# A gated-state attention with a low-rank mixer: order of the first batch, its idle products, and of the loads up to unit 5

## The chip, the cores and the metric

One NeuronCore of a Trainium2 chip. The metric is the device time of one execution in microseconds (us). A core has five engines with an instruction stream each: TensorE (PE; its weight loads are shown apart as PEld), VectorE (DVE), ScalarE (ACT), GpSimd (POOL) and SyncE (SP), which here only issues DMA transfers.

## What is computed

```python
f = 1 / (1 + exp(-f_logit))                     # (B, H, S, D) = (4, 8, 768, 48)
for t in range(S):
    state = f[:, :, t, :, None] * state + k[:, :, t, :, None] * v[:, :, t, None, :]
    y[:, :, t] = q[:, :, t] @ state             # per batch and head
x = y as (B, S, H*D) = (4, 768, 384)
u = x + ((x.T @ U) @ V).T                       # U: (768, 32), V: (32, 768), mixes the 768 positions
out = u + relu(u @ w_ch1) @ w_ch2               # 384 -> 1536 -> 384
```

All in float32, except that the four weight matrices come in as float64.

## The kernel before

The attention runs over 16 units, two heads of one batch each; units 0 to 3 are batch 0, units 4 to 7 batch 1, and so on. The 768 positions are cut into 12 chunks of 64, taken two at a time as 6 blocks of 128. Within a chunk the recurrence becomes products: q times the product of gates from the chunk's start (Y), k times the inverse of it or the product to its end (X), a masked score matrix, and a state handed from chunk to chunk by a scan on VectorE.

For units 0 to 3 the gates are worked out through logarithms. `prepare(n)` gives five pieces, which `front(n, ...)` calls by the names gates, read_back, keep, keys, queries:

- `logs` ("gates"): VectorE bounds the f tile (L697), ScalarE takes Exp (L698) and Ln (L699), over all six blocks at once.
- `log_sums` ("read_back"): TensorE multiplies each block with the constant `later`, six products of 130 columns (L705, twelve instructions).
- `keep_logs` ("keep"): ScalarE makes X (L717), Y (L718) and two small tiles from the sums.
- `keys` and `queries`: TensorE transposes k or q (L678), VectorE multiplies with X or Y (L690).

`attend(n)` gives the second half, which `rear(n, ...)` calls: kept (transposes of kz, L864, and ScalarE's copy kb, L868), spread (L874), states (products with v, L885, and the copy `added`, L892), scores (L837), mask (L850), scan (L907), read (q times the states, L924), inner (scores times v, L942, and the copy into x, L948).

The mixer follows for each batch: the low-rank part (L217 to L248 for batch 0), turn (L261 and L262), the first product pz with its relu on ScalarE (L273, L283), and the second. Mixer work of batch 0 runs beside units 4 to 8, and likewise later; from batch 1 on the second product is done with fewer multiplications.

Weights come as float64, in tiles of 384 KB. For each, SP issues the load (L82, a tile `w_raw`, of which there are four, or `zw`), ScalarE splits it (L91, L92), VectorE shapes it in three steps (L98 to L100) in the tile `w_y`, of which there are two, and GpSimd adds the parts (L101). In the list `weights`, 0 to 2 are U and V (`early` is 3), 3 to 14 the twelve tiles of w_ch1, then twelve of w_ch2. `ahead_by(early + FIRST, weights)` issues the load nine places ahead of the tile that is converted.

The order on TensorE, VectorE and ScalarE is the program's order throughout (`manual_schedule`); SP's order is the program's until `written.close()`. `load(n, names)` issues the loads of unit n: two transfers of 144 KB for each of f, k and q (L563), and three for v (L563, L556). Units 0, 2, 4 use the slots in `late`, units 1, 3, 5 those in `other`; there are three v tiles. `busy(n)` issues idle products that nothing reads. In `late`, slice 3 is `ends`, slices 4 and 5 are X of units 0 to 3 in turn.

Of the kernel before, what the change touches and what calls it, by code (L numbers as in the profile page):

```python
# [14 lines left out]
AF = mybir.ActivationFunctionType  # L15
# [12 lines left out]
FLOOR = -40.0  # L28
# [459 lines left out]
def factored_path(ctx, tc, q, k, v, f_logit, moe_U, moe_V, moe_w_ch1, moe_w_ch2, out, ok):  # L488
# [82 lines left out]
                        in_=head[:, :, part * NB : part * NB + n_ch],  # L571
                    )

    load(0, "f")
    load(1, "f")
    load(0, "k", "q", "v")

    nc.scalar.preload_act_table_set("natural_log_exp_and_others")

# [81 lines left out]
    def prepare(n):  # L661


        T = units[n] = {}
        b = n // HP
        r, f = raw[n % 2], fz[n % 2]
        by_chunk = f[:, 0:S].rearrange("p (c t) -> p c t", t=C)

        def follow(nm):

            if n >= HP and n + 2 < NU:
                load(n + 2, nm)

        def on_tensor(nm):

            pt = ps_big.tile([P, 2, 512], F32, name="pt", tag="big")
            for c in range(NBL):
                nc.tensor.transpose(  # L678
                    pt[:, 2 * c // NBL, c % (NBL // 2) * P : (c % (NBL // 2) + 1) * P],
                    nat[n % 2][nm][:, c].rearrange("p h d -> p (h d)"), ident,  # L680
                )
            return pt[:, :, 0 : G * C].rearrange("p a (c t) -> p a c t", t=C)

        def halves(t):
            return t[:, 0:S].rearrange("p (a c t) -> p a c t", a=2, t=C)

        def operand(nm, of):
            t = T[nm] = kz[n % 2][:, C:] if nm == "k" else two.tile([P, S], F32, name="qT")
            if n < TURNED:
                nc.vector.tensor_tensor(halves(t), on_tensor(nm), halves(T[of]), ALU.mult)  # L690
            else:
                turned(t, r[nm])
                nc.vector.tensor_tensor(t, t, T[of], ALU.mult)

        def logs():
            fn = nat[n % 2]["f"][:, :, :, 0:D]
            nc.vector.tensor_single_scalar(fn, fn, FLOOR, ALU.max)  # L697
            nc.scalar.activation(fn, fn, AF.Exp, scale=-1.0)  # L698
            nc.scalar.activation(fn, fn, AF.Ln, bias=1.0)  # L699

        def log_sums():
            pt = T["sums"] = ps_big.tile([P, 2, 512], F32, name="pt", tag="big")
            for c in range(NBL):
                o = c % (NBL // 2) * (P + 2)
                nc.tensor.matmul(  # L705
                    pt[:, 2 * c // NBL, o : o + P + 2],
                    lhsT=nat[n % 2]["f"][:, c].rearrange("p h d -> p (h d)"), rhs=later, start=True, stop=True,
                )

        def keep_logs():  # L710
            by_block = T["sums"][:, :, 0 : NBL // 2 * (P + 2)].rearrange("p a (c t) -> p a c t", t=P + 2)

            def blocks_of(t):
                return t.rearrange("p (a c t) -> p a c t", a=2, t=P)

            T["X"], T["Y"] = late[:, 4 + n % 2, :], fz[n % 2][:, 0:S]
            nc.scalar.activation(blocks_of(T["X"]), by_block[:, :, :, 0:P], AF.Exp, scale=-1.0)  # L717
            nc.scalar.activation(blocks_of(T["Y"]), by_block[:, :, :, 0:P], AF.Exp)  # L718
            nc.scalar.activation(
                least[:, n, :].rearrange("p (a c s) -> p a c s", a=2, s=2), by_block[:, :, :, P : P + 2], AF.Exp, scale=-1.0  # L720
            )
            nc.scalar.copy(wholes[n % 2][:, 1:NCH], least[:, n, 1:NCH])

        def gates():
            f0 = T["f0"] = two.tile([P, NCH], F32, name="f0")
            if n < TURNED:
                pt = on_tensor("f")
                nc.scalar.activation(halves(f)[:, :, :, 1:C], pt[:, :, :, 1:C], AF.Sigmoid)
                nc.scalar.activation(f0.rearrange("p (a c) -> p a c", a=2), pt[:, :, :, 0], AF.Sigmoid)
                follow("f")  # L730
                return
            fT = late[:, 6, :]
            turned(fT, r["f"])
            follow("f")
            fv = fT.rearrange("p (c t) -> p c t", t=C)
            nc.scalar.activation(by_chunk[:, :, 1:C], fv[:, :, 1:C], AF.Sigmoid)  # L736
            nc.scalar.activation(f0, fv[:, :, 0], AF.Sigmoid)

        def keep():
            X = T["X"] = late[:, 4, :]  # L740
            nc.vector.tensor_tensor_scan(  # L741
                backwards(X, S - 1, S), backwards(f, S, S), backwards(ends, S - 1, S), 0.0,
                ALU.mult, ALU.add,
            )
            X0 = X.rearrange("p (c t) -> p c t", t=C)[:, :, 0]
            nc.scalar.copy(least[:, n, :], X0)
            X1 = two.tile([P, NCH], F32, name="X1")
            nc.vector.tensor_single_scalar(X1, X0, LEAST, ALU.max)
            nc.vector.reciprocal(starts.rearrange("p (c t) -> p c t", t=C)[:, :, 0], X1)
            whole = wholes[n % 2]  # L750
            nc.vector.tensor_tensor(whole[:, 1:NCH], T["f0"][:, 1:NCH], X0[:, 1:NCH], ALU.mult)

        def keys():
            operand("k", "X")
            follow("k")

        def read():
            Y = T["Y"] = late[:, 5, :]
            nc.vector.tensor_tensor_scan(Y, f[:, 0:S], starts, 0.0, ALU.mult, ALU.add)  # L759

        def queries():
            operand("q", "Y")
            follow("q")

        if n < HP:
            return [logs, keep_logs, keys, log_sums, queries]
        return [gates, keep, keys, read, queries]
# [190 lines left out]
    def front(n, *names):  # L958

        if n >= NU:  # L960
            return []
        if n not in ahead:
            ahead[n] = dict(zip(("gates", "keep", "keys", "read_back", "queries"), prepare(n)))
        return [ahead[n].pop(nm) for nm in names]

    def rear(n, *names):

        if not 0 <= n < NU:
            return []
        if n not in here:  # L970
            here[n] = dict(zip(("kept", "states", "scan", "scores", "read", "inner", "mask", "spread"), attend(n)))
        return [here[n].pop(nm) for nm in names if nm in here[n]]
# [53 lines left out]
    with tc.manual_schedule(engines={nc.vector.engine, nc.scalar.engine}):  # L1026
# [1 line left out]

        idle = ps_mm.tile([P, 512], F32, name="idle", tag="mm")

        def busy(n):
            for _ in range(n):
                nc.tensor.matmul(idle[:, 0:DM], lhsT=ident, rhs=ends[:, 0:DM], start=True, stop=True)  # L1033

        written = ExitStack()
        written.enter_context(tc.manual_schedule(engines={nc.sync.engine}))
        busy(2)
        for piece in front(0, "gates", "read_back", "keep"):
            piece()
        load(2, "f")  # L1040
        load(1, "k", "q", "v")
        loads = ahead_by(early + FIRST, weights)
        halves, join = [[w[i] for w in weights[:early]] for i in (2, 3)]
        done, rest = slice(0, 2 * (HP - 1) * D), slice(2 * (HP - 1) * D, DM)
# [10 lines left out]
        for n in range(HP):  # L1055
            last = n + 1 == HP
            pieces = rear(n - 1, "scan", "mask") + front(n, "keys")
            if last:
                pieces += join[:1]
            elif n < 2:  # L1060
                pieces += [lambda: busy(2)]
            pieces += rear(n, "spread") + rear(n - 1, "read") + rear(n, "kept")
            if last:
                pieces += halves[1:2] + front(n, "queries") + rear(n - 1, "inner") + [held] + join[1:2] + rear(n, "states")
                pieces += halves[2:] + rear(n, "scores")
            else:
                pieces += rear(n - 1, "inner") + front(n + 1, "gates") + front(n, "queries") + rear(n, "states", "scores")
                pieces += (halves[:1] if n + 2 == HP else []) + front(n + 1, "read_back", "keep")
            for piece in pieces:
                piece()  # L1070
            if n == 0:
                load(3, "f")
                load(2, "k", "q", "v")
                for load_w in weights[:early]:
                    load_w[0]()
            elif n == 1:
                load(3, "k", "q", "v")
                for load_w in weights[early : early + 2]:
                    load_w[0]()
        m = mixer(0)  # L1080
        low_rank_of, added_up_of, mix_of, warm = m.some
        for piece in rear(n, "scan", "mask") + join[2:]:
            piece()
        load(HP + 1, "f", "k", "q", "v")
        for load_w in weights[early + FIRST : early + FIRST + early]:
            load_w[0]()
        written.close()
        low_rank_of(done)
        warm(2)
        loads[early]()  # L1090
        nc.vector.memset(starts, 0.0)
        for t in fz:
            nc.vector.memset(t, 0.0)
        for piece in rear(n, "read"):
            piece()
        added_up_of(done)
# [6 lines left out]
        mix_of(rest)  # L1103
        warm(3)
        loads[early + 1]()
        loads = loads[early + 2 :]

        start = m.before[3:5] + m.firsts[0:1] + m.before[5:]
# [398 lines left out]
```

## Time and profile before

| | us |
|---|---|
| three runs | 482.61, 483.89, 484.61; median 483.89 |
| profiled execution | 483.7 |
| its span, first to last instruction | 482.0 |
| TensorE busy | 462.7 |
| VectorE busy | 345.3 |
| ScalarE busy | 179.8 |
| GpSimd busy | 36.3 |
| first unit's log sums start | 6.61 |
| first product of the mixer (L273) starts | 49.98 |

The span is what the profile shows; the time of the same execution is 1.7 us longer. A profile line of the timeline has start, length, engine, line of the kernel, operation, the tiles written and read, shapes and count, and in brackets how long the engine sat idle before and what ended it. Matmuls overlap, so lengths of TensorE lines are a little longer than their distance.

### The profile page before, as it was taken

How to read it: one execution, taken by the hardware profiler on the slowest of the kernel's cores; microseconds unless marked ns; L12 is line 12 of the kernel's file. 1: busy time of each engine (PE TensorE's matmuls, PEld its weight loads, DVE VectorE, ACT ScalarE, POOL GpSimd, SP SyncE). 2: the span in 40 equal slices, each digit the busy share in tenths (PEclk: the TensorE clock that was granted, in tenths of full speed). 3: DMA queues.
4: the chain of work that ended last, by engine and by line, in shares of the span. 5: the costliest groups of instructions: out<-in, count | busy, mean ns of one | idle time of the engine just before them, and what ended most of it. 6: DMA issues, size and time to landing. Idle time of an engine off the chain costs nothing.

```text
span 482.0 us, 12801 instructions
## 1 busy us (share of the span) xinstructions
PE 462.7 (96%) x5561; PEld 399.8 (83%) x5561; DVE 345.3 (72%) x555; ACT 179.8 (37%) x335; POOL 36.3 (8%) x48
## 2 busy tenths in 40 slices
PE   6999989999999899999999999999999999999995
PEld 4886877886666468799899888899979999999995
DVE  2568769878999755757766646997896886858642
ACT  4675567573444313424342414542321311212200
POOL 2002435443000000000000000000000000000000
PEclk9999999999999999999999999999999999999999
DMA  9977985658787521153426200100000000000001
GB/s 144 160 161 205 171 234 151 161 132 114 114 122 110 98 42 26 26 75 72 64 29 114 43 31 4 28 3 20 18 0 1 33 2 18 18 0 34 1 33 40
DMA packets 158680, 34.36 MB, mean 71 GB/s; under 512 B 149206, under 2 KB 157078, under 8 KB 158614
## 3 DMA queue, kind: packets, MB, share of 16 engines
q1 hardware_dynamic: 158614, 33.44, 37.3%
q8 instruction: 46, 0.75, 0.7%
q14 instruction: 20, 0.16, 0.1%
HBM read 28.70 MB, written 4.72 MB: 69 GB/s over the span
## 4 chain that ended last, share of the span: by engine, by line
PE 70%; DVE 13%; ACT 4%; DMA 4%; SPq 3%; issue 3%; POOL 1%; DVEq 0%; POOLq 0%; ACTq 0%
PE pw L327 26%; PE pz L273 16%; PE pp L425 12%; PE y L942 2%; DVE late L759 2%; PE sc L837 2%; PE y L924 2%; SPq L569 2%; PE po L298 2%; PE put L261 1%; PE pt L705 1%; DVE added L907 1%; PE pt L864 1%; PE idle L1033 1%; DVE late L741 1%
## 5 line engine op out<-in xcount | busy, mean ns | idle before, releaser
L273 PE MATMUL pz<-uT,w 128*128 128x256 f32 x504 | 114.5, 382 | 4.1 <-ACT z_all L283 3.8
L273 PEld LDWEIGHTS pz<-uT,w 128*128 128x128 f32 x504 | 93.8, 190 | 18.0 <-ACT z_all L283 4.8
L327 PE MATMUL pw<-w,z_all 128*128 128x192 f32 x216 | 37.7, 329 | 0.0
L327 PE MATMUL pw<-zw,w_raw 128*128 128x192 f32 x216 | 37.3, 327 | 0.0
L327 PEld LDWEIGHTS pw<-zw,w_raw 128*128 128x128 f32 x216 | 35.2, 190 | 0.7 <-DVE w_raw L197 0.6
L327 PEld LDWEIGHTS pw<-w,z_all 128*128 128x128 f32 x216 | 35.0, 190 | 0.7
L101 POOL TENSOR_TENSOR w<-w_y,w_r 128x384 int32<-128x384 int32 x24 | 31.7, 1320 | 42.4 <-DVE w_y L100 39.3
L283 ACT ACTIVATE z_all<-pz 128x512 f32<-128x512 f32 x33 | 19.7, 597 | 32.7 <-PE pz L273 32.6
L425 PE MATMUL pp<-v_nat,late 128*128 128x128 f32 x224 | 28.8, 275 | 0.0
L425 PEld LDWEIGHTS pp<-v_nat,late 128*128 128x128 f32 x224 | 27.0, 192 | 0.0
L418 ACT ACTIVATE other<-other 128x512 f32<-128x512 f32 x18 | 11.3, 632 | 39.9 <-DVE other L197 39.9
L912 ACT COPY st<-added 128x576 f32<-128x576 f32 x12 | 14.7, 1225 | 30.5 <-DVE added L907 30.5
L298 PE MATMUL po<-w,z_all 128*128 128x384 f32 x72 | 24.9, 493 | 1.2 <-DVE o L197 1.2
L298 PE MATMUL po<-w,zw 128*128 128x384 f32 x72 | 25.3, 496 | 0.0
L741 DVE TENSOR_TENSOR_SCAN late<-fz,late 128x768 f32<-128x768 f32 x12 | 21.1, 1756 | 4.0 <-ACT fz L736 3.6
L850 DVE TENSOR_TENSOR A<-sc,causal 128x768 f32<-128x768 f32 x16 | 15.1, 946 | 10.8 <-PE sc L837 10.8
L98 DVE TENSOR_SCALAR w_y<-w_y 128x384 f32<-128x384 f32 (+3 forms) x27 | 12.5, 465 | 12.9 <-ACT w_y L91 12.6
L298 PEld LDWEIGHTS po<-w,z_all 128*128 128x128 f32 x72 | 13.3, 190 | 10.1 <-DVE o L197 1.8
L298 PEld LDWEIGHTS po<-w,zw 128*128 128x128 f32 x72 | 13.1, 190 | 9.7 <-issue 1.2
L759 DVE TENSOR_TENSOR_SCAN late<-fz,other 128x768 f32<-128x768 f32 x12 | 21.0, 1747 | 0.2
L418 ACT ACTIVATE z_all<-z_all 128x512 f32<-128x512 f32 x12 | 7.6, 632 | 32.8 <-DVE z_all L197 32.8
L892 ACT COPY added<-ds 48x576 f32<-48x576 f32 (+1 forms) x28 | 17.8, 635 | 3.3 <-PE ds L885 3.2
(215 smaller groups left out, 846.0 us busy)
## 6 DMA issues: line engine op xcount, KB each, us to landing
w_raw<-in_moe_w_ch_dram SPq DMA_DIRECT2D x18, 384.0 KB, 3.4
out_dram<-o SPq DMA_DIRECT2D x24, 192.0 KB, 2.0
v_nat<-in_v_dram SPq DMA_DIRECT2D x16, 144.0 KB, 3.3
v_nat<-in_v_dram SPq DMA_DIRECT2D x32, 72.0 KB, 3.2
zw<-in_moe_w_ch_dram SPq DMA_DIRECT2D x6, 384.0 KB, 5.7
late<-in_f_logit_dram SPq DMA_DIRECT2D x10, 96.0 KB, 3.2
late<-in_k_dram SPq DMA_DIRECT2D x10, 96.0 KB, 2.7
late<-in_q_dram SPq DMA_DIRECT2D x10, 96.0 KB, 2.9
```

The lines of the kernel that those rows point to most:

```text
L101: nc.gpsimd.tensor_tensor(dst.bitcast(I32), shaped(y.bitcast(I32)), shaped(r), ALU.add)
L273: nc.tensor.matmul(pm[:, i * 2 * P : (i + 1) * 2 * P], lhsT=w1[:, m, o : o + P], rhs=uT[a][:, m, :], start=(m == 0), stop=(m == NDC - 1))
L283: nc.scalar.activation(z[a, c][:, k : k + 2, :].rearrange("p i t -> p (i t)"), pm, AF.Relu)
L298: nc.tensor.matmul(pm, lhsT=z[a, i // NI][:, i % NI, s * P : (s + 1) * P], rhs=w2[:, i, :], start=(i == 0), stop=(i == NFC - 1))
L327: nc.tensor.matmul(pm[:, n * HM : (n + 1) * HM], lhsT=lhs[:, i, :], rhs=rhs[:, i, :], start=(i == 0), stop=(i == NI - 1))
L418: nc.scalar.activation(dst, dst, AF.Relu, scale=float(SIGNS[n]))
L425: nc.tensor.matmul(pm[:, i, r * P : (r + 1) * P], lhsT=room["w"](wn)[:, r * P : (r + 1) * P], rhs=x_node(a, xn), start=((xn, wn) == of[0]) ...
L741: nc.vector.tensor_tensor_scan(backwards(X, S - 1, S), backwards(f, S, S), backwards(ends, S - 1, S), 0.0, ALU.mult, ALU.add,)
L759: nc.vector.tensor_tensor_scan(Y, f[:, 0:S], starts, 0.0, ALU.mult, ALU.add)
L850: nc.vector.tensor_tensor(T["A"], sc[:, :, 0 : NBL * C].rearrange("p h (c i) -> p h c i", i=C), causal.unsqueeze(1).unsqueeze(1).broadcast ...
L892: nc.scalar.copy(added[r, 1:].rearrange("p (e c s) -> p e c s", c=NBL, s=2), ds[r, :, 0 : NBL * D].rearrange("p s (c e) -> p e c s", e=D),)
L912: nc.scalar.copy(st, states.rearrange(by_e, c=NCH))
```

## The change

Five things are changed, all in the way from the first load to the first products of the mixer.

1. A tile of zeros, `blank` (slice 5 of `late`, 384 columns), is the first memset of VectorE, and `busy` multiplies it with itself in place of `ident` and `ends`. `busy(3)` stands at the start in place of `busy(2)`; the `busy(2)` in units 0 and 1 goes, and unit 0 gets one idle product of 256 columns.
2. Unit 0's logarithms are taken in two halves of three blocks, and X of unit 0 in two halves.
3. In unit 0, queries, kept and scores come ahead of `log_sums` of unit 1, with the queries straight after the keys, the scores ahead of the states.
4. The loads are in another order: f, k, q of unit 0, then f of unit 1, then v of unit 0; k and q of a unit ahead of f of the next one; U, and V with the second part of `early`, behind unit 2; three weight tiles (list places 9 to 11) ahead of unit 5's loads in place of behind them.
5. The clearing of `starts` and `fz` moves from between the conversions of weights 3 and 4 to behind that of 4.

```diff
+    blank = late[:, 5, 0 : 3 * P]
+    nc.vector.memset(blank, 0.0)
+    load(0, "f", "k", "q")
     load(1, "f")
-    load(0, "k", "q", "v")
+    load(0, "v")
...
         def logs():
-            fn = nat[n % 2]["f"][:, :, :, 0:D]
-            nc.vector.tensor_single_scalar(fn, fn, FLOOR, ALU.max)
-            nc.scalar.activation(fn, fn, AF.Exp, scale=-1.0)
-            nc.scalar.activation(fn, fn, AF.Ln, bias=1.0)
+            m = 2 if n == 0 else 1
+            parts = [nat[n % 2]["f"][:, i * NBL // m : (i + 1) * NBL // m, :, 0:D] for i in range(m)]
+            for fn in parts:
+                nc.vector.tensor_single_scalar(fn, fn, FLOOR, ALU.max)
+            for fn in parts:
+                nc.scalar.activation(fn, fn, AF.Exp, scale=-1.0)
+                nc.scalar.activation(fn, fn, AF.Ln, bias=1.0)
...
-            nc.scalar.activation(blocks_of(T["X"]), by_block[:, :, :, 0:P], AF.Exp, scale=-1.0)
+            for a in (slice(0, 1), slice(1, 2)) if n == 0 else (slice(0, 2),):
+                nc.scalar.activation(blocks_of(T["X"])[:, a], by_block[:, a, :, 0:P], AF.Exp, scale=-1.0)
...
-        def busy(n):
+        def busy(n, cols=DM):
             for _ in range(n):
-                nc.tensor.matmul(idle[:, 0:DM], lhsT=ident, rhs=ends[:, 0:DM], start=True, stop=True)
+                nc.tensor.matmul(idle[:, 0:cols], lhsT=blank[:, 0:P], rhs=blank[:, 0:cols], start=True, stop=True)
...
-        busy(2)
+        busy(3)
         for piece in front(0, "gates", "read_back", "keep"):
             piece()
+        load(1, "k", "q")
         load(2, "f")
-        load(1, "k", "q", "v")
+        load(1, "v")
...
-            elif n < 2:
-                pieces += [lambda: busy(2)]
+            if n == 0:
+                pieces += front(n, "queries") + rear(n, "spread", "kept") + [lambda: busy(1, 2 * P)]
+                pieces += front(n + 1, "gates") + rear(n, "scores", "states") + front(n + 1, "read_back", "keep")
+                for piece in pieces:
+                    piece()
+                load(2, "k", "q")
+                load(3, "f")
+                load(2, "v")
+                continue
...
-            if n == 0:
-                load(3, "f")
-                load(2, "k", "q", "v")
-                for load_w in weights[:early]:
+            if n == 1:
+                weights[0][0]()
+                load(3, "k", "q")
+                for load_w in weights[1:early]:
                     load_w[0]()
-            elif n == 1:
-                load(3, "k", "q", "v")
+                load(3, "v")
                 for load_w in weights[early : early + 2]:
                     load_w[0]()
...
-        load(HP + 1, "f", "k", "q", "v")
         for load_w in weights[early + FIRST : early + FIRST + early]:
             load_w[0]()
+        load(HP + 1, "f", "k", "q", "v")
         written.close()
         low_rank_of(done)
         warm(2)
         loads[early]()
-        nc.vector.memset(starts, 0.0)
-        for t in fz:
-            nc.vector.memset(t, 0.0)
...
         loads[early + 1]()
+        for t in [starts] + fz:
+            nc.vector.memset(t, 0.0)
```

Unit 0's old order on TensorE was keys, two idle products, kept, queries, states, scores, then the log sums of unit 1.

More of the change, by code (lines that the diff above doesn't have):

```diff
@@ L572, in load @@
                     )
-    load(0, "f")
+    blank = late[:, 5, 0 : 3 * P]
+    nc.vector.memset(blank, 0.0)
+    load(0, "f", "k", "q")
     load(1, "f")
-    load(0, "k", "q", "v")
+    load(0, "v")
     nc.scalar.preload_act_table_set("natural_log_exp_and_others")
```

## The prediction

> **What bounds the kernel now.** I read the page's first and second part, then the chain of waits in order of time, then the timelines of TensorE, ScalarE and the SP queue for the first 75 us, and last the waits of TensorE after 48 us.
>
> ```profile
> PE 462.7 (96%) x5561; PEld 399.8 (83%) x5561; DVE 345.3 (72%) x555; ACT 179.8 (37%) x335; POOL 36.3 (8%) x48
> PE   6999989999999899999999999999999999999995
> DMA  9977985658787521153426200100000000000001
> ...
> PE pz L273 <- ACT z_all L283: 3.8, 3, 1.8
> ```
>
> TensorE is the bound: 96% of the span, and after the first batch its waits are few (the last line: three waits, 3.8 us, for the relu that empties the output of the mixer's first product). So TensorE's stream after about 48 us is nearly solid, and whatever is taken away ahead of it, or out of a hole in it, should come off the end one for one. There are two such places: the first batch (0 to 48 us), which is a chain of short steps, and a hole at 62 us.
>
> The first batch, TensorE's timeline (start, length, then what; L705 is the product `log_sums`, once per unit, and so marks the units):
>
> ```profile
> 3.89 2.93 PE L1033 MATMUL idle<-late,ident 128*128 128x384 f32 x4 [3.89 <-POOL ident masks.py:199]
> 6.61 2.79 PE L705 MATMUL pt<-later,late 128*128 128x130 f32 x12
> ...
> 14.67 1.61 PE L705 MATMUL pt<-later,other 128*128 128x130 f32 x12
> ...
> 16.77 1.46 PE L1033 MATMUL idle<-late,ident 128*128 128x384 f32 x4
> ...
> 23.63 1.61 PE L705 MATMUL pt<-later,late 128*128 128x130 f32 x12
> ...
> 31.68 1.61 PE L705 MATMUL pt<-later,other 128*128 128x130 f32 x12
> ```
>
> The reader is to see three things. The first L705 group takes 2.8 us, the later ones 1.6: the same twelve instructions at half pace. The distances of the L705 groups are 8.06, 8.96 and 8.05 us; the long one is unit 1, where idle products stand at 16.77 in front of the read of the states (L924, at 18.15). And TensorE does nothing until 3.89, waiting for `ident` from GpSimd.
>
> The hole, from the timelines of TensorE, ScalarE and SP:
>
> ```profile
> 63.66 5.45 PE L273 MATMUL pz<-uT,w 128*128 128x256 f32 x24 [1.76 <-ACT z_all L283]
> ...
> 73.31 2.86 PE L273 MATMUL pz<-uT,w 128*128 128x256 f32 x12 [0.96 <-ACT z_all L283]
> ...
> 62.13 0.54 ACT L91 ACTIVATE w_y<-w_raw 128x384 f32<-128x384 f32 x1 [5.44 <-DMA w_raw<-in_moe_w_ch_dram]
> ...
> 51.57 1.15 SPq L563 DMA_DIRECT2D other<-in_f_logit_dram  x2
> ...
> 57.74 6.76 SPq L82 DMA_DIRECT2D w_raw<-in_moe_w_ch_dram  x5
> ```
>
> TensorE waits 1.76 us for a relu; ScalarE had waited 5.44 us for a weight tile with the relu queued behind; SP issued that tile at 57.74 because unit 5's loads (51.57 to 57.69) stood ahead of it. The 0.96 us at 73.31 is what is left of the same jam: the relu there stood behind the gates of unit 4, themselves late because ScalarE worked off its queue.
>
> [...] L705 has 0.215 us per instruction until 9.40, the transposes after it 0.11. [...] here the q, k, v, f rows are 192 B and move at about 165 GB/s when several are queued (7 to 9 us), the weight tiles at about 345 (59 to 64 us). So the order of loads matters in the first batch.
>
> **The change part by part.** All against the profiled execution: 483.7 us with a span of 482.0, which is 0.2 below the median of 483.89.
>
> Warm-up. The zero tile is half of L606's columns (0.70 us for 768), so 0.35 on VectorE from 0.90; it delays only VectorE's constants, which end at 2.51 with the engine free until 4.63. Idle products then start at about 1.3 instead of 3.89; six instructions of 0.64 (the pace at 3.89) end at 5.15. [...] I carry both, 2.58 or 1.55 us.
>
> Logarithms in halves. The f tile of unit 0 lands as before (4.63). A half costs VectorE about 0.28 (of 0.46) and an activation 0.40 (L228's copy of 288 columns); so the first half is ready at 5.82, the second at about 6.5, where the whole is ready now at 6.52. Log sums end at 7.4 (warm) or 8.4 (cold) against 9.40. X in halves costs 0.3 more on an idle ScalarE, and the second half ends 0.55 after the sums.
>
> Loads of unit 0. k and q move ahead of unit 1's f. Issue to landing is 4.2 to 4.3 for k: second half now at 7.9, then at about 6.1; q at about 8.0 instead of 9.6; f of unit 1 at 9.7 instead of about 6.6, where it is first used after 9.9. The five loads of 295 KB at 165 GB/s from 2.6 us on still put v of unit 0 at about 12.1, as now.
>
> Queries ahead, filler cut. kz ends at 9.2 (warm) or 10.3 (cold), qT 0.9 to 1.4 later (13.77 now), scores at 11.1 or 12.6. Then `states` needs v: it starts at 12.1 or 12.6, takes 0.75, and unit 1's log sums start at 12.95 (warm) or 13.6 (cold: unit 1's logarithms end then) against 14.74 in the chain. Gain 1.8 or 1.1. What is late next is v's transfer; without it the warm gain would be about 0.9 more.
>
> Unit 1. The two idle products (1.29 us) ahead of L924 go. Its distance should become that of unit 2, 8.05, plus 0.3 because the mask of unit 0 now stands just ahead of kz: unit 2's log sums at 21.3 against 23.70. Gain in all 2.4 warm, 1.7 cold; I take 2.2. Its v (issue about 0.8 earlier, landing about 19.2) is wanted at 19.2; no room, 0.5 if it is late. Units 2 and 3 keep their 8 us. SP's reordering there (U behind unit 2, unit 3's k and q ahead of V) leaves each load before its use by my count: k of unit 3 about 1 us, the others 1 to 2.
>
> Weight tiles between units 4 and 5. SP issues them at 51.5 (49.3 with the shift) instead of 57.74, so they land at about 54.3; ScalarE comes to the first at 56.7 (54.5 shifted). Both 1.76 and 0.96 go: 2.7. Unit 5's six loads and three behind them in kind go back by about 1.8 us of issue; its f is first used by TensorE at 82.6, so nothing is late.
>
> Clearing of `starts` and `fz`. 2.2 us of VectorE (0.70 + 1.51) leave 43.4 to 45.6, where the five additions to x wait for them but TensorE's next transpose doesn't start later for it, and go to 49.6, into the conversion of weights. Two conversion buffers make ScalarE wait for GpSimd; walking the queue I find the copy of the third turned block 0.15 late for TensorE and the rest covered (a product pair takes 2.6 us, a conversion about 2). Cost 0.15, between 0 and 1.
>
> Sum: 2.2 + 2.7 - 0.15 = 4.75; 483.7 - 4.75 = 479.0. Everything after 75 us only moves ahead, since units 4 and on and TensorE's fillers are started by the same stream.
>
> **The rivals.** First, the weights still come late for ScalarE (the queue is fuller when the first batch is shorter, or the cleared tiles cost their 2 us): only the first part stays, 483.7 - 2.2 = 481.5. For it: the landing at 54.3 has only 0.2 us to spare. Against it: a late tile of a few tenths costs only those.
>
> Second, the first batch is held by its transfers: the DMA row stands at 7 to 9 tenths there and v of units 0 and 1 lands just in time. Then only the hole goes: 483.7 - 2.6 = 481.1. Against it: SP waits for free buffers at 8.65 and 16.34 now, which the new order fills.
>
> Third, slower: with the filler cut from 2.58 to 0.43 us in units 0 and 1, TensorE has only 1.9 us of work (kept, filler, scores) between 8.7 and 12.1. [...] a unit's 7.2 us of products take 14.4, 6.4 more than the slack of 0.8 hides. One cold unit gives 479.0 + 6.4 = 485.4, two 491.8; I enter 488. It decides the sign from about 5.3 us of products at half rate on. Against it: TensorE never rests longer than 1.2 us at a stretch in my walk, and no L705 group after the first is slow.
>
> **How the numbers follow.** The forecast 0.60, late weights 0.16, transfers 0.12, the cold clock 0.12. The predicted time is that of the first, 479.0; its own range is 477.0 (v early, warm, no cost of the clearing) to 480.5 (cold start, 0.5 for v, 1 for the clearing). To hold eight in ten I reach to the first two rivals and a little of the third: 476.8 to 483.5. What a measurement here can tell from no change is about 0.5%, 2.4 us: faster below 481.5, slower above 486.3. Faster 0.73 (0.58 + half of each of the first two rivals), within 0.18, slower 0.09.
>
> **What would show it.** Right: a first idle product near 1.3 us; log sums of units 1 and 2 near 13.0 and 21.3; `states` of unit 0 waiting for v; no wait of L273 near 60 us. Wrong: log sums of unit 2 after 22.5, L705 at 0.215 us per instruction in unit 1 or later, a DMA wait of L91 that outlasts 55 us, or new waits of TensorE between 75 and 180 us, which would mean that the vector work and not TensorE set the pace there.

## The result, and the profile after

| | before | changed |
|---|---|---|
| median, us | 483.75 (7 runs, 482.61 to 484.61) | 480.69 (7 runs, 479.83 to 481.94) |
| ratio, 95% interval | | 0.9941 [0.9924, 0.9959] |
| span of the profiled execution | 482.0 | 479.0 |
| log sums of units 1, 2 and 3 start | 14.67, 23.63, 31.68 | 12.92, 22.05, 30.35 |
| first product of the mixer (L273) starts | 49.98 | 49.49 |
| kept of unit 4 done, next L273 starts | 79.86 | 77.03 |

The kernel became 3.1 us faster, by the median, where 4.75 were forecast. The last three rows tell where. Unit 1 starts 1.75 us earlier, as forecast; the gain shrinks to 1.58, 1.33, and to 0.49 at the first product of the mixer, where 2.2 were forecast. Between the first product and 77.03 it grows by 2.34, where 2.55 were forecast, and from there it stays to the end of the span (3.0).

The timeline of TensorE of the changed kernel for the first batch (start, length, engine, line, operation, tiles, shapes, count, and in brackets the idle time before and what ended it):

```profile
1.39 4.21 PE L1039 MATMUL idle<-late 128*128 128x384 f32 x6 [1.39 <-DVE late L575]
6.01 2.09 PE L710 MATMUL pt<-later,late 128*128 128x130 f32 x12 [0.41 <-issue]
...
15.98 1.24 PE L930 MATMUL y<-st,qT 48*64 48x48 f32 x44 [0.80 <-DVE A L856]
...
19.31 1.28 PE L891 MATMUL ds<-v_nat,kb 64*64 64x48 f32 x48
20.59 0.68 PE L843 MATMUL sc<-qT,kz 48*64 48x64 f32 x29
21.56 0.56 PE L843 MATMUL sc<-qT,kz 48*64 48x64 f32 x19 [0.29 <-issue]
...
26.33 1.16 PE L948 MATMUL y<-v_nat,A 64*64 64x48 f32 x48
...
30.35 1.16 PE L710 MATMUL pt<-later,other 128*128 128x130 f32 x8
32.35 0.61 PE L710 MATMUL pt<-later,other 128*128 128x130 f32 x4 [0.83 <-issue]
```

The idle products start at 1.39 and the log sums (L705 of before is L710 here) at 6.01, as forecast. Then look at the groups that are cut in two. The scores of unit 1 stop after 29 of 48 for 0.29 us, the log sums of unit 3 after 8 of 12 for 0.83 us, and "issue" says that nothing the profile shows ended the wait. L948 of unit 2 takes 1.16 where it takes 0.92 elsewhere, and `states` of unit 1 (L891) 1.28 instead of 0.92. The profile of the kernel before has no such gap; these are its scores of unit 1, all 48 in one piece:

```profile
22.77 0.93 PE L837 MATMUL sc<-qT,kz 48*64 48x64 f32 x48 [0.37 <-ACT late L699]
```

But the same first batch was profiled again in the first experiment below, which leaves it as it was, and there these scores do stop, after 25 of 48:

```profile
22.52 0.59 PE L837 MATMUL sc<-qT,kz 48*64 48x64 f32 x25 [0.37 <-ACT late L699]
23.48 0.57 PE L837 MATMUL sc<-qT,kz 48*64 48x64 f32 x23 [0.37 <-issue]
```

So the stop is not a thing of the new order alone, and one profile is one draw. The first product of the mixer starts at 49.98, 50.02 and 50.15 in the three profiles of the old first batch that were taken with all its loads and none added, and anywhere from 49.25 to 50.68 in the six with the changed one. What the first batch is worth is therefore read from the times below, and the 0.49 of this pair of profiles is not taken as its size.

The hole: first the product that ends the stretch in TensorE's timeline of the kernel before (it begins with the one at 49.98), then the timelines of TensorE, SP and ScalarE of the changed kernel:

```profile
79.86 2.86 PE L273 MATMUL pz<-uT,w 128*128 128x256 f32 x12
```

```profile
49.49 2.83 PE L273 MATMUL pz<-uT,w 128*128 128x256 f32 x12 [0.33 <-ACT uT L262]
...
55.72 5.45 PE L273 MATMUL pz<-uT,w 128*128 128x256 f32 x24 [0.15 <-ACT uT L262]
61.01 0.82 PE L680 MATMUL pt<-ident,late 128*128 128x128 f32 x6
61.66 5.35 PE L273 MATMUL pz<-uT,w 128*128 128x256 f32 x24
...
70.48 2.86 PE L273 MATMUL pz<-uT,w 128*128 128x256 f32 x12 [0.23 <-ACT z_all L283]
...
77.03 2.86 PE L273 MATMUL pz<-uT,w 128*128 128x256 f32 x12
```

```profile
51.39 1.68 SPq L82 DMA_DIRECT2D w_raw<-in_moe_w_ch_dram  x3
...
61.78 1.61 SPq L82 DMA_DIRECT2D w_raw<-in_moe_w_ch_dram  x3
```

```profile
57.88 0.57 ACT L91 ACTIVATE w_y<-w_raw 128x384 f32<-128x384 f32 x1 [0.44 <-POOL w L101]
...
66.09 0.55 ACT L91 ACTIVATE w_y<-w_raw 128x384 f32<-128x384 f32 x1 [0.61 <-DMA w_raw<-in_moe_w_ch_dram]
```

The three tiles are issued at 51.39 and ScalarE no longer waits for the first of them; the wait of 1.76 us is gone and that of 0.96 has become 0.23. A new one of 0.15 stands before the third turned block (the clearing, forecast 0.15). Together that is 2.34 less, the whole of what this stretch gained. What is left is the next weight tile, issued at 61.78 behind unit 5's loads, for which ScalarE waits 0.61.

### The profile page after: what moved, and what is told of

Read it like the earlier page. It is cut to its first block, busy times and chain, and to the rows that moved or that the text cites. A ratio compares the mean times of both kernels' runs of the same rounds, so it can differ in the third digit from the quotient of the medians.

```text
span 479.0 us, 12800 instructions
## 1 busy us (share of the span) xinstructions
PE 462.1 (96%) x5557; PEld 399.0 (83%) x5557; DVE 346.0 (72%) x557; ACT 181.0 (38%) x338; POOL 36.1 (8%) x48
## 4 chain that ended last, share of the span: by engine, by line
PE 75%; DVE 11%; ACT 5%; issue 3%; DMA 3%; SPq 1%; POOL 0%; DVEq 0%; ACTq 0%
PE pw L327 26%; PE pz L273 20%; PE pp L425 12%; PE sc L843 2%; PE y L948 2%; PE y L930 2%; DVE late L765 2%; PE po L298 2%; DVE late L747 1%; DVE added L913 1%; PE put L261 1%; PE pt L870 1%; PE ds L891 1%; PE pt L710 1%; PE pu L207 1%
## 5 line engine op out<-in xcount | busy, mean ns | idle before, releaser
L273 PE MATMUL pz<-uT,w 128*128 128x256 f32 x504 | 114.7, 382 | 1.8 <-ACT z_all L283 1.3
L273 PEld LDWEIGHTS pz<-uT,w 128*128 128x128 f32 x504 | 93.7, 190 | 15.8 <-ACT z_all L283 2.1
L327 PE MATMUL pw<-w,other 128*128 128x192 f32 x108 | 18.6, 327 | 0.0
```

Of the source, the lines that this page charges most:

```text
L273: nc.tensor.matmul(pm[:, i * 2 * P : (i + 1) * 2 * P], lhsT=w1[:, m, o : o + P], rhs=uT[a][:, m, :], start=(m == 0), stop=(m == NDC - 1))
L327: nc.tensor.matmul(pm[:, n * HM : (n + 1) * HM], lhsT=lhs[:, i, :], rhs=rhs[:, i, :], start=(i == 0), stop=(i == NI - 1))
```

## The experiments

The theory after the result: (1) the hole and the first batch are two separate gains; (2) units 1 to 3 are held by transfers, so that what unit 0 gains is taken back there. The rivals: that the hole closes only because the batch ends earlier; that the new order of the engines' work stretches the units; that the profiled execution was an unlucky one. All ratios are to the kernel before, run on the same chip beside the experiment.

**The two halves, each alone.** The first has of the change only this:

```diff
-        load(HP + 1, "f", "k", "q", "v")
         for load_w in weights[early + FIRST : early + FIRST + early]:
             load_w[0]()
+        load(HP + 1, "f", "k", "q", "v")
...
-        nc.vector.memset(starts, 0.0)
-        for t in fz:
-            nc.vector.memset(t, 0.0)
...
         loads[early + 1]()
+        for t in [starts] + fz:
+            nc.vector.memset(t, 0.0)
```

> The kernel before with only the three weight tiles ahead of unit 5's loads and the clearing of starts and fz behind weight 4. Theory A (the hole at 62 us is worth its 2.7 us by itself, and the first batch gives next to nothing at its end): 2.3 to 2.7 us less than before, ratio 0.9945 to 0.9955; no wait of L273 over 0.3 us between 55 and 70. Theory B (the hole closes only because the first batch ends earlier, so that the weights and ScalarE fall in step): less than 1.5 us gain.

Measured: 480.86 against 483.73, ratio 0.9942 [0.9924, 0.9961], 2.87 us. The waits that remain in it are 0.16 and 0.32, a little above the bound set. The hole is worth nearly the whole change by itself.

The second is the changed kernel with these lines put back.

> The changed kernel with the weight tiles and the clearing put back where they were before. Theory A (the first batch's gain is lost again in units 1 to 3): 0.2 to 0.8 us less than before, ratio 0.998 to 1.0; log sums of unit 1 near 12.9, first product of the mixer within 0.7 of 49.98; the wait of ScalarE for the weight tile as long as before. Theory B (the 1.8 us at unit 1 reach the mixer in most executions, and the profiled one was unlucky): about 1.5 to 2 us less than before.

Measured: 483.0 against 483.73, ratio 0.9986 [0.9975, 0.9997], 0.73 us; first product at 49.61, 0.37 earlier than before. This is the upper end of theory A, and theory B's 1.5 to 2 is outside the interval. In its profile the log sums of unit 3 again stop after 8 of 12 instructions, for 0.76 us. ScalarE waits 4.81 us for the weight tile at 61.13, 0.6 less than before. The two parts add up to 3.6, the change gave 3.1, within what these intervals can tell.

**A quarter of the first batch's transfers taken away.** In this kernel q of units 0 to 3 isn't loaded; it is set to zero once. The engines do the same instructions, on zeros where q was.

```diff
         for nm in names:
+            if nm == "q" and n < HP:
+                continue
...
-            nc.gpsimd.memset(t[:, :, :, D:PAD], 0.0)
+            nc.gpsimd.memset(t if nm == "q" else t[:, :, :, D:PAD], 0.0)
```

> The changed kernel without the loads of q for units 0 to 3 (their q is set to zero once by GpSimd), so that a quarter of the first batch's bytes and issues is gone and all engines have the same work. Theory A (units 1 to 3 are stretched by transfers: v of unit 1 late[...]): the distances of the log sums fall from 9.13, 8.3 (plus 0.83 inside L710) and 8.2 to about 8.3, 8.05 and 7.2, the first product of the mixer comes 1.3 to 2 us earlier, at about 47.8, and the end with it. Theory B (the new order of the engines' work stretches them: mask ahead of kz, read behind the mask): the distances stay, and the first product stays within 0.5 of 49.5.

Measured: 478.63, ratio 0.9902 [0.9865, 0.9938], 5.1 us below before. TensorE's timeline:

```profile
12.53 1.61 PE L712 MATMUL pt<-later,other 128*128 128x130 f32 x12
...
21.06 1.61 PE L712 MATMUL pt<-later,late 128*128 128x130 f32 x12
...
29.12 1.61 PE L712 MATMUL pt<-later,other 128*128 128x130 f32 x12
...
47.23 2.83 PE L273 MATMUL pz<-uT,w 128*128 128x256 f32 x12 [0.33 <-ACT uT L262]
```

The distances are 8.53 and 8.06, no group is cut, and the first product comes 2.26 us earlier than in the changed kernel. With the transfers out of the way the new order gives what the prediction's walk gave it (8.35 and 8.05). So in the changed kernel it is transfers that stretch the units, and not the order of the engines' work. Of that order only a part remains: the read of the states (L932 in this kernel) still waits 0.80 for the mask, and the first distance is 0.2 over the forecast. The time agrees: 478.63 is 1.9 below that of the changed kernel with the clearing on GpSimd, run beside it (480.53, further down). What the kernel before would gain from the same cut of loads was not run.

**More transfers in the kernel before.** Six loads of 144 KB that nothing reads go into z_all, two behind each of units 0 to 2.

```diff
+        def more(n):
+            for par in range(2):
+                o = (2 * n + par) * NBL * D
+                nc.sync.dma_start(
+                    out=junk[:, o : o + NBL * D].rearrange("p (c d) -> p c d", d=D),
+                    in_=f_logit[B - 1, 2 * n + par].rearrange("(c p) d -> p c d", p=P),
+                )
...
+            if n < 3:
+                more(n)
```

> The kernel before with six more loads of 144 KB (rows of 192 B, into z_all, which is first written at 52 us; nothing reads them), two behind each of units 0 to 2, one and a half times a unit's v. Theory A (units 1 to 3 are held by transfers[...]): 864 KB at 165 GB/s is 5.2 us; the slack of the old order takes some 2, so the first product of the mixer comes 2 to 4 us later than 49.98, with waits of DMA or gaps of TensorE that nothing in the kernel explains. Theory B (the batch is a chain of engines and the queue has room): under 0.7 us.

Measured: 485.86 against 484.17, ratio 1.0062 [1.0038, 1.0086]; first product at 52.09, 2.1 later. The nine runs spread from 485.05 to 489.84. The three longest (488.76 and up) had a mean granted clock of 0.985 to 0.991, the others 0.996 to 0.999; none of the three was profiled, so where they lost it is open. TensorE's timeline of unit 2 in the profiled execution:

```profile
25.34 0.85 PE L678 MATMUL pt<-ident,late 128*128 128x128 f32 x6 [0.28 <-DMA late<-in_k_dram]
...
27.90 0.68 PE L942 MATMUL y<-v_nat,A 64*64 64x48 f32 x30
29.42 0.55 PE L942 MATMUL y<-v_nat,A 64*64 64x48 f32 x18 [0.85 <-issue]
```

Both kinds of loss appear in the old order too with a fuller queue: a tile that comes late (k of unit 2, 0.28 us), and a cut group whose wait nothing names (0.85). (The cut group appeared there once without added loads, as shown above.)

**The unnamed gaps.** Where a group is cut can be counted in TensorE's matmul instructions from the first one on. In the changed kernel the stops come after 345 (29 scores of unit 1) and 596 (8 log sums of unit 3); the extra-loads kernel stops after 472, and the stretched L948 of the changed kernel spans 438 to 486. The distances are 127 and 124. In the first experiment, whose first batch has another order, the 25 scores of unit 1 end after 345 too. The next test was a second profile of the changed kernel, and a kernel that has two matmul instructions fewer at its start: unit 0's logarithms and X whole, and the idle products at the start as before.

```diff
-            m = 2 if n == 0 else 1
+            m = 1
...
-            for a in (slice(0, 1), slice(1, 2)) if n == 0 else (slice(0, 2),):
+            for a in (slice(0, 2),):
...
-        busy(3)
+        for _ in range(2):
+            nc.tensor.matmul(idle[:, 0:DM], lhsT=ident, rhs=ends[:, 0:DM], start=True, stop=True)
```

> The changed kernel once more, for a second profile of it and for the comparison with the next three on one chip. Theory A [...]: gaps again at the 29th of the 48 score instructions of unit 1, about two thirds into L948 of unit 2 or at the 8th of the 12 L710 instructions of unit 3, as long as or shorter than before, and nowhere else without a named cause. Theory B (the gaps are chance): other places. Time 480.7, ratio 0.993 to 0.995.

> The changed kernel with unit 0's logarithms and X whole and the idle products at the start as before (two, with ident). Theory A (transfers hold units 1 to 3): unit 1's log sums come about 1.3 later, near 14.2, but the first product of the mixer within 0.6 of 49.5 and the time within 0.6 us of the changed kernel. Theory B (what unit 0 gains is passed on): 1 to 1.5 us more than the changed kernel.

> The changed kernel with unit 0's logarithms and X whole and the start as before, once more beside the changed kernel. Theory A (transfers take most of unit 0's gain): 0.2 to 0.7 us above the changed kernel. Theory B (passed on in full): 1 to 1.5 us above it.

The kernel with whole logarithms, second profile, TensorE's timeline:

```profile
20.60 0.69 PE L843 MATMUL sc<-qT,kz 48*64 48x64 f32 x31
21.46 0.50 PE L843 MATMUL sc<-qT,kz 48*64 48x64 f32 x17 [0.18 <-issue]
...
29.94 1.38 PE L710 MATMUL pt<-later,other 128*128 128x130 f32 x10
31.87 0.38 PE L710 MATMUL pt<-later,other 128*128 128x130 f32 x2 [0.54 <-issue]
```

The stops have moved from 29 to 31 and from 8 to 10: again after 345 and 596 matmul instructions. Its first profile stopped in the scores after 31 (0.44 us) and not in the log sums. The second profile of the changed kernel stopped after 8 of 12 (0.56 us); its scores were hardly cut but took 1.30, and its L948 of unit 2 took 1.10. The places are thus fixed in the instruction stream, and how long the stop is, or whether there is one, depends on the execution. What holds TensorE there was not shown: the lines put the waits, 0.18 to 0.92 us, down to "issue" alone. The page's third part lists a queue of its own for instructions:

```profile
q8 instruction: 46, 0.75, 0.7%
```

In the changed kernel one of these 46 packets falls between 19.0 and 19.2 and one between 29.6 and 29.8, 2.4 to 2.8 us before the stops end (21.56 and 32.35). That names no cause: in the profile of the kernel before one falls between 20.2 and 20.4, 2.4 to 2.6 us ahead of the scores at 22.77, which are not cut.

The time of these kernels: the changed one again 480.22, 0.9933 [0.9911, 0.9956]; whole logarithms 481.79 against 484.17, 0.9959 [0.9945, 0.9974], and in the second series 480.4, 0.9938 [0.9919, 0.9958]. Beside the changed kernel that is 0.2 us slower, by the first series some 0.8, between its two theories; halves and early start are worth something between 0.2 and 0.8, and the intervals can't say where. In the first profile unit 1's log sums start at 14.06 and the first product at 49.81: 1.14 us later than in the changed kernel at unit 1, 0.32 later at the mixer. One reason for such differences is seen in the log sums of unit 0: with the start as before they take 1.64 us in the second profile of this kernel and 2.76 in the first; what decides between the two the profiles don't show. The early start doesn't ensure the shorter time either: 1.70 to 2.94 us over the profiles that have it. In the slowest of them, that of the last experiment below, unit 1's log sums start at 14.32 instead of 12.92.

**The order of the loads in units 1 to 3.** The changed kernel with the order of before for units 1 to 3, U and V:

```diff
-        load(1, "k", "q")
         load(2, "f")
-        load(1, "v")
+        load(1, "k", "q", "v")
...
-                load(2, "k", "q")
                 load(3, "f")
-                load(2, "v")
+                load(2, "k", "q", "v")
+                for load_w in weights[:early]:
+                    load_w[0]()
...
-                weights[0][0]()
-                load(3, "k", "q")
-                for load_w in weights[1:early]:
-                    load_w[0]()
-                load(3, "v")
+                load(3, "k", "q", "v")
```

> The changed kernel with the loads of units 1 to 3 and of U and V in the order of before (f of the unit after next first, U and V ahead of unit 3); unit 0's order stays. Theory A (the number of bytes holds units 1 to 3, not their order): within 0.7 us of the changed kernel. Theory B (the new order puts v too late and keeps the queue fuller): 1 to 2 us less than the changed kernel, first product near 48.3.

Measured: 481.4 against 484.17, ratio 0.9944 [0.9931, 0.9957], level with the changed kernel's 0.9941. By the time the order is worth nothing that can be told; theory B is out. Its profiled execution shows what the new order avoids (TensorE's timeline, then the busy time by stretch, with the granted clock in the column behind POOL):

```profile
16.80 0.85 PE L680 MATMUL pt<-ident,other 128*128 128x128 f32 x6 [2.19 <-DMA other<-in_k_dram]
...
21.16 1.54 PE L680 MATMUL pt<-ident,other 128*128 128x128 f32 x6
```

```profile
17.00:25.20 8.20, 8.20 (x212) 7.36 (x210) 2.58 (x4) 3.72 (x7) 0.00 (x0) 0.58 0.93 148
```

TensorE waits 2.19 us for unit 1's k, and then runs at a granted clock of 0.58 on average for 8 us; six transposes of unit 1 take 1.54 where they take 0.87 in the changed kernel. A clock this low is what the third rival of the prediction supposes, met in one execution of a kernel that isn't the change; that the wait brought it down was not shown.

**Clearing on GpSimd.** In the changed kernel `nc.gpsimd.memset` in place of `nc.vector.memset` for starts and fz.

> The changed kernel with starts and fz cleared by GpSimd, which rests there, in place of VectorE. Theory A (the clearing in the middle of the weight conversions holds ScalarE's copy of the third turned block): the 0.3 us between the second and third first products go, 0.2 to 0.4 us less than the changed kernel, ratio to before about 0.9935. Theory B (GpSimd takes longer and holds the additions of weights 5 and 6): 0 to 1 us slower than the changed kernel.

> The changed kernel with the clearing on GpSimd, beside the changed kernel on one chip. Theory A (the holes between the third turned block and the second keys close): from the first product of the mixer to the 79th us 0.5 to 0.9 us less, and the time 0.4 to 0.9 us below the changed kernel's. Theory B: no difference beyond 0.3 us.

Measured: 480.53, 0.9929 [0.9901, 0.9957], and in the second series 480.43, 0.9933 [0.9914, 0.9952], beside the changed kernel's 480.22. The wait for the third turned block is gone in both profiles, but the time isn't lower: a miss. The first profile lost 1.22 us to a late v tile in unit 2 and 1.00 in unit 3, where it names a copy of ScalarE (L1056); the second still waits 0.40 for a relu at 70.00.

**The old first batch with the clearing on GpSimd:**

> The kernel before with the weight tiles ahead of unit 5's loads and the clearing on GpSimd, so everything of the changed first batch left out. Theory A (the changed first batch is worth 0.3 to 0.7 us, the rest lies in the hole): 0.3 to 0.7 us above the changed kernel with the clearing on GpSimd, about level with the changed kernel. Theory B (the changed first batch is worth nothing): level with the changed kernel with the clearing on GpSimd.

Measured: 481.52, 0.9951 [0.9935, 0.9968]: 1.1 above the changed kernel with the clearing on GpSimd and 1.3 above the changed one. That would put the changed first batch at or above what theory A gave it, but the intervals overlap, and part of the difference lies elsewhere: in this profile ScalarE waits 1.89 us for the weight tile at 67.36, TensorE 1.40 in the end.

**A fourth weight tile ahead.** With the three tiles ahead, ScalarE still waits for the next one (list place 12) in six of nine profiles, 0.45 to 1.89 us. So, with the clearing on GpSimd:

```diff
-        loads = ahead_by(early + FIRST, weights)
+        loads = ahead_by(early + FIRST + 1, weights)
...
-        for load_w in weights[early + FIRST : early + FIRST + early]:
+        for load_w in weights[early + FIRST : early + FIRST + early + 1]:
```

> The changed kernel with the clearing on GpSimd and a fourth weight tile (list place 12) ahead of unit 5's loads, every later tile issued one place earlier. Theory A (what is left of the hole is ScalarE's wait for that tile): no wait of ScalarE for a weight tile between 60 and 70, no wait of L273 after the third turned block, 0.3 to 0.8 us below the changed kernel, ratio to before 0.991 to 0.993. Theory B (the tile of place 13 now blocks SP, which waits for the buffer of place 9, and unit 6's f comes late): level or up to 1 us slower than the changed kernel.

Measured: 479.58 against 483.84, ratio 0.9912 [0.9897, 0.9928]. TensorE's timeline:

```profile
50.39 2.83 PE L273 MATMUL pz<-uT,w 128*128 128x256 f32 x12 [0.33 <-ACT uT L262]
53.71 7.94 PE L273 MATMUL pz<-uT,w 128*128 128x256 f32 x36
62.14 5.35 PE L273 MATMUL pz<-uT,w 128*128 128x256 f32 x24
67.98 5.35 PE L273 MATMUL pz<-uT,w 128*128 128x256 f32 x24
73.81 2.76 PE L273 MATMUL pz<-uT,w 128*128 128x256 f32 x12
77.02 2.86 PE L273 MATMUL pz<-uT,w 128*128 128x256 f32 x12
```

No bracket is left after the first: 26.63 us from the first product to the one at 77.02, 27.54 in the changed kernel, 29.88 before. ScalarE has no wait for a weight tile there either. But the first GpSimd profile, with three tiles ahead, had these 26.63 us too, and the second 27.30, with the wait of 0.40. The kernel with four tiles is the fastest by the median of the kernels that compute everything, 4.3 us below before. Its interval only just overlaps that of the changed kernel's first series and overlaps more with its second, so a gain of about 1 us over the changed kernel is likely and not settled.

## Why the prediction came out as it did

The measured 480.69 lies in the wide range, but just outside the forecast's own range of 477.0 to 480.5. The hole came out as argued; the first batch did not, and it is the allowance for the rivals that held the result.

- The start and the logarithms in halves: right. The first idle product at 1.39 (1.3), log sums of unit 0 over at 8.10 (7.4 or 8.4), of unit 1 at 12.92 (12.95 or 13.6). Warm and cold stand for the two paces of the log sums in the profile of before, 1.61 us for twelve instructions and 2.79; the granted clock is 1.00 there in both stretches, and what sets the pace was not shown.
- "What is late next is v's transfer", for unit 0: not in the changed kernel, where `states` starts at 12.04 straight behind the scores. In the kernel with the old order of units 1 to 3 it was, by 0.17. The sum given for v's landing (five loads of 295 KB at 165 GB/s from 2.6 us on) makes 11.5, not 12.1.
- "Gain in all 2.4 warm, 1.7 cold; I take 2.2": this is the term that was mis-sized. Unit 1 took 9.13 us where I had 8.35, unit 2 8.30 where I had 8.05, and unit 3 lost 0.83 inside its log sums. The batch kept 0.49 in this profile, 0.73 alone by the time. The profile of unit 1 has the mask's wait (0.80; I had 0.3 for its effect), v at 19.70 where it was wanted at 19.31, and the stop of 0.29. I had seen that v had "no room", with 0.5 in the range but nothing in the sum, and had no term for the stops, which no line of the profile of before showed. Without q's loads the gain of 2.2 is there (2.75 at the first product, fewer loads included).
- "Both 1.76 and 0.96 go: 2.7", less 0.15: right in mechanism and nearly in size, 2.34 in the profile and 2.87 by the time alone. I had not followed the next tile, place 12, behind unit 5's loads: 0.61 of ScalarE and 0.23 of TensorE. The weight tiles moved at about 345 GB/s only from 61 to 64 us; the mean from 59 to 64 was 289.
- "Everything after 75 us only moves ahead": right; 2.83 at 77.03, 3.0 at the end.
- The rivals: the second (the first batch held by its transfers, 481.1) is nearer to 480.69 than the forecast of 479.0 is; it had 0.12. The wide range rested on it. Late weights: no. The clock: 0.999 and 0.997 on average in the changed kernel's two profiles, but 0.58 for 8 us in another kernel's. That little work on TensorE brings it down was the author's estimate; nothing in the profile of before shows it.
- The signs: an idle product at 1.39, unit 1's log sums at 12.92 (13.0) and no wait near 60 us came as listed for right; unit 2's log sums lie between the two marks (22.05; right was 21.3, wrong after 22.5), and `states` did not wait for v. Of those for wrong one came by its wording, a DMA wait of L91 that outlasts 55 us (0.61, over at 66.09), for a tile the prediction had not followed.

## What to carry to other kernels

A queue of loads can hold an engine by a tile that comes late: here k of unit 1, for 2.19 us in the kernel with the old order of units 1 to 3. The stops, up to 0.92 us each, are a loss of another kind, whose cause was not shown. Where a chain of engines is shortened while its loads stay, ask first how early the last load of each stage can land. And when weight loads are moved past other loads, follow the tile behind the last one moved: here that one step, with the clearing out of VectorE's way, gave about another microsecond by the median. And one profile of a stretch with many transfers is one draw: take a second before explaining a few tenths of a microsecond.

## What the runs showed of the hardware

TensorE stopped at fixed places in its instruction stream, after 345, 472 and 596 matmul instructions, for up to 0.92 us (the last experiment, after 345). It did so in three different streams: the changed kernel (0.29 and 0.83 us), the one with two instructions fewer at its start (0.18 and 0.54), and the old first batch (0.37 us with its own loads, 0.85 with six added). It did not do so in every execution: no stop at these places in the profile of before, nor with q's loads left out, nor after 596 in the last experiment, which loads everything. So the one profile without q's loads doesn't show that the loads cause the stops, and what causes them was not shown.

In the kernel with the old order of units 1 to 3, after a wait of 2.19 us the granted clock was 0.58 on average for 8 us (17.0 to 25.2), with TensorE busy throughout, and 1.00 from there to 33.0. In the kernel before it was 1.00 from 62 to 74 us, after the wait of 1.76 us (the hole). That the longer wait is what brought it down was not shown.
